# A planned attention and feed-forward kernel: VectorE takes score tiles earlier, half chunks become slices, two weights' homes become buffers, and the plan is made by other rules

## The chip, the cores and the metric

The kernel runs on one core of one Trainium2 chip. A core has TensorE (in profiles PE, its weight loads PEld), ScalarE (ACT), VectorE (DVE), GpSimd (POOL) and SyncE (SP), each with a queue of its own that runs in order. The metric is the device time of one execution in microseconds (us), lower is better.

## The reference

The input is 2048 rows of 640. After a layer norm, an attention with 32 query heads of 20 dimensions that share one key and one value head, and a feed-forward part with silu, 1728 wide, are added to the input.

```python
def reference(A_x, A_wq, A_wk, A_wv, A_wo, B_x, B_w1, B_w2):
    x = A_x                                      # (1, 2048, 640)
    xn = _layernorm(x, axis=-1)
    def _A_ref(x, wq, wk, wv, wo):               # H = 32, Dh = 20
        q = (x @ wq).reshape(B, S, H, Dh).transpose(0, 2, 1, 3)
        k, v = x @ wk, x @ wv                    # one head, Dh wide
        p = _softmax(einsum("bhqd,bkd->bhqk", q, k) * (Dh ** -0.5), axis=-1)
        o = einsum("bhqk,bkd->bhqd", p, v)
        return o.transpose(0, 2, 1, 3).reshape(B, S, H * Dh) @ wo
    def _B_ref(x, w1, w2):                       # w1 640x1728, w2 1728x640
        return _silu(x @ w1) @ w2
    return x + _A_ref(xn, A_wq, A_wk, A_wv, A_wo) + _B_ref(xn, B_w1, B_w2)
```

## The kernel before

**Tiles.** The 2048 queries are four chunks of 512 (QC), the 32 heads eight groups of four (NG, HG), so there are 32 pairs of chunk and group, and each walks over 16 key tiles of 128 (KT). One score tile is 128 keys by 512 queries of one head and fills one PSUM bank; there are 2048. A head's 20 dimensions lie in one of four groups of 32 partitions, so the scores of four different heads can run side by side on TensorE as four matmuls of 32 rows (L1052, function `s_mm`). One to four of them together are called a burst here, and a visit is the time TensorE spends with bursts between other work.

**Two ways to the exponential.** ScalarE takes two or three score tiles from neighbouring banks in one instruction (L1140). VectorE takes one tile at a time (L1336): it adds a bias to the score and writes an int16 whose bits, read as bf16, are a power of two with a straight line between powers. Four such tiles, the four heads of one key tile, are a batch and lie in one buffer of `z_t`. Two shifted copies of the batch are made, by GpSimd (L1375) or VectorE (L1380), and the three are multiplied with three weighted copies of the values, which makes up for the straight lines. So a batch costs three groups of value matmuls (L1175, four matmuls of 32 columns side by side) where ScalarE's tiles cost one. There are five buffers in `z_t`: three of their own and two halves of `zx`.

**Other work on TensorE.** Queries (`q_job`, 20 jobs of 5 groups), hidden layer (`h_job`, `h_pair`), outputs (`out_job`, 24 jobs, and `y_job`, 8 jobs for the last chunk of queries) go through `col_mm` (L434), four matmuls of 32 columns side by side. A hidden job is evicted by ScalarE's tanh (L756) and VectorE (L759), a query job by VectorE (L679), which also sends its rows to their places by DMA (L692), an output job by VectorE (L878 and L893). Of the 14 hidden chunks of 128 the last has 64 live rows; two query chunks share one job for it, so the even one's rows lie in the lower half of the partitions and the odd one's in the upper half, and the other half is zero. An output matmul group can be cut into four slices of 32 rows (`row_slice`, `row_mm`, L441) that run beside a score burst whose heads leave a row group free; slices of one job wait for each other.

**The prologue.** Until `pro` is empty, TensorE takes in order the transposes of the normed rows (L582, copied by L594 or ScalarE L591), the keys (L608, copied by ScalarE L618), the values (L632, L640) and the first two query jobs. In this time ScalarE's banks are fixed: three and two by turns (`ABUFS`), and other jobs have two banks (`XBANKS`); VectorE takes no score tiles.

**The order of the work.** `build` is a planner: it holds a cost for every instruction and a clock for every engine, and always gives the engine that is furthest behind its next instruction. For TensorE, `step_pe` sorts what is ready by kind (s scores for ScalarE, d a score tile for VectorE, r a slice, z a slice left over, p and pd value matmuls, m and l jobs) in an order that depends on the rules: numbers such as `keep`, `hold`, `need`, `stay`. They start from `BASE`, and every 10,000 ns of planned time the next letter of `PLAN` picks an entry of `RULES` that changes some of them. `emit` turns the plan into five queues and semaphore waits, so the chip runs each queue in the planned order. Bank 7 always accumulates the values; the other seven are handed out as they come free.

Of the kernel before, what the change touches and what calls it, by code (L numbers as in the profile page):

```python
# [14 lines left out]
P = 128  # L15
# [21 lines left out]
UB = 7  # L37
XBANKS = (5, 6)
VECTOR_EXP = True
# [41 lines left out]
YC = (0, 0, 3, 3)  # L81
EARLY = 0
WLATE = ("w2a", "wo")
# [12 lines left out]

BASE = dict(hold2=0, bnd=4, pj=6000.0, rows=0, rowmin=3, lagmax=6, lagp=0, lagj=6, openlag=5, late=-0.02, lead=0.01, leadmax=0.02, need=460.0, hold=300.0, dwant=600.0, slack=550.0, dnow=400.0, hungry=0.0, patience=0.0, keep=460.0, open=2, zcap=9, stay=0.0, homes=1, want=1, claim=6)
RULES = dict(a={}, b=dict(keep=0.0), c=dict(lagp=3), d=dict(lagp=5), e=dict(lagp=0), f=dict(patience=200.0), g=dict(dwant=0.0),
             h=dict(zcap=4), i=dict(zcap=3), j=dict(homes=0), k=dict(leadmax=-1.0, lead=-1.0), l=dict(lead=0.08, leadmax=0.1),
             m=dict(need=560.0), n=dict(hold=0.0), o=dict(stay=460.0), p=dict(open=1), q=dict(slack=400.0), r=dict(hungry=1000.0), s=dict(claim=9), t=dict(open=3), u=dict(claim=4), v=dict(want=2), w=dict(slack=700.0), x=dict(hold2=4), y=dict(bnd=0), z=dict(pj=-1e9), A=dict(rows=0), B=dict(rows=2, rowmin=2), C=dict(pj=2000.0), D=dict(openlag=3), E=dict(pj=8000.0), F=dict(hold2=3), G=dict(rows=1))  # L100
PLAN = "aaanGtxBBExhEhmxadrBBzraCBBEGqtrztfFzrqhwnpofocotyxddmGjvmpBaBitntqo"

# [16 lines left out]
class Op:  # L119
    __slots__ = ("eng", "fn", "occ", "lat", "pre", "reads", "writes", "prio", "mode", "slots",  # L120
                 "start", "fin", "done", "deps", "inc", "job", "first", "last", "gate", "on_commit", "seq", "name",
                 "dma_sem", "dma_val", "port", "run", "cut", "ends", "sync")

    def __init__(self, eng, fn, occ, lat=0.0, pre=(), reads=(), writes=(), prio=5.0, mode=None, slots=None,
                 job=None, gate=None, on_commit=None, name=""):
        self.eng = eng
        self.fn = fn
        self.occ = occ
        self.lat = lat
        self.pre = list(pre)  # L130
        self.reads = list(reads)
        self.writes = list(writes)
        self.prio = prio
        self.mode = mode
# [12 lines left out]
        self.port = False  # L147
        self.cut = None
        self.sync = None
        self.ends = (True, True)  # L150

# [167 lines left out]
def build(nc, A_x, A_wq, A_wk, A_wv, A_wo, B_x, B_w1, B_w2, out, stack):  # L319
# [346 lines left out]
    def q_job(qc, k):  # L666
# [5 lines left out]
        for c in range(DC):  # L672
# [4 lines left out]
                     and all(o.done for o in q_piece.get(ql - NQS, ())), dyn=True)  # L677
        xq_read[qc].append(job)
        op = Op("dve", lambda v: v.tensor_scalar_mul(q_st[:, st, :], bk(job.bank), QSCALE), t_dve(512), 140,  # L679
                pre=[job.ready], writes=[res("qst", st)], prio=0.4, job=job)  # L680
# [24 lines left out]
    hc_op = {}  # L705
    xq_read = {k: [] for k in range(QC)}
    t_users = {}
    out_done = {}

    def h_pair(qb):  # L710
# [13 lines left out]
        for q in (qa, qb):  # L724
            xq_read[q].append(job.ops[-1])
        ts = (qb * FC + fk) % 2
        tp = [t_users[ts]] if ts in t_users else []
# [15 lines left out]
    def h_job(qc, fk):  # L743
# [8 lines left out]
        job = pe_job(f"h{qc}_{fk}", mms, 1100, gate=lambda: qc < 2 or all((qc - 2, i) in out_done for i in range(QTP)), dyn=True)  # L752
        xq_read[qc].append(job)
        ts = (qc * FC + fk) % 2
        tp = [t_users[ts]] if ts in t_users else []
# [14 lines left out]
    def load_xres(qc):  # L770
        for i in range(QTP):
# [94 lines left out]
    def out_job(qc, i, hf):  # L866
        e0, e1 = hf * HALF, (hf + 1) * HALF
        mms = ffn_mms(qc, i, e0, e1, True, False) + o_mms(qc, i, e0, e1, False, True)
        job = pe_job(f"out{qc}_{i}_{hf}", mms, 19 * 140, gate=lambda: (qc, NG - 1) in pack_op, dyn=True)
        sl = (QTP * qc + i) % 3  # L870

# [17 lines left out]
    def y_job(qc, i, hf):  # L889
        e0, e1 = hf * HALF, (hf + 1) * HALF  # L890
        mms = ffn_mms(qc, i, e0, e1, True, not YC[i]) + o_mms(qc, i, e0, e1, False, True, range(YC[i]))
        job = pe_job(f"y{qc}_{i}_{hf}", mms, (14 + YC[i]) * 140, dyn=True)
        op = Op("dve", lambda v: v.scalar_tensor_tensor(out=yx[:, i, e0:e1], in0=bk(job.bank, 0, HALF), scalar=0.5,  # L893
                                                        in1=xres[:, i, e0:e1], op0=ALU.mult, op1=ALU.add),
                t_dve(HALF), 140, pre=[job.ready, xres_op[(qc, i)]] + [norm_op[n] for n in range(NT)] + [out_done[(qc - 1, t)] for t in range(QTP)], reads=[res("xres", i)], writes=[res("yx", i, hf)], prio=0.3, job=job)
        y_op[(i, hf)] = op
        job.consumers = [op]
        return job
# [108 lines left out]
    ru = SimpleNamespace(**BASE)  # L1007
    att = {"sgroup": 0, "pgroup": 0, "n": 0, "items": 0, "value": 0.0}
    NGR = QC * NG
# [307 lines left out]
    def yx_users(zi):  # L1317
        return [wqp0] if zi >= NZ0 else []

# [212 lines left out]
    def ready_to_make(m):  # L1532
# [11 lines left out]
        if m[0] == "y":  # L1544
            if (m[1], m[2]) not in xres_op or any((m[1], fk) not in hc_op for fk in range(FC)):
                return False
            return all((m[1] - 1, t) in out_done for t in range(QTP)) and all((m[1], g) in pack_op for g in range((YC[m[2]] * P - 1) // (HG * DH) + 1))
        if m[0] == "h" and m[2] == FC - 1 and m[1] == 3 and not all((0, i) in out_done for i in range(QTP)):
# [104 lines left out]
    def pe_candidates():  # L1653
# [10 lines left out]
        prog = (att["items"] + HG * len(batches)) / total_items  # L1664
        lead = misc_done[0] / misc_total - PACE * prog - ENDLEAD * max(0.0, prog - ENDFROM) / (1.0 - ENDFROM)
        behind = lead < ru.lead or recent() < BUSY
# [28 lines left out]
    def row_slice(piece):  # L1695

        job = piece.job
        if not job.dyn or not ru.rows or sc.pe_mode != "s" or sc.pe_set is None or sc.t["pe"] > sc.pe_set[2] + 1.0 or job.burst == sc.pe_set[0]:
            return None
        busy = sc.pe_set[1]  # L1700
        pick = next(((x, r) for x in job.rest for r in job.rest[x] if r not in busy), None)
        if pick is None and len(job.rest) < ru.rows and len(piece.mms) > ru.rowmin:
            x = next((x for x in list(piece.mms)[-2:0:-1] if x.cut is not None and all(p.done for p in x.pre)), None)
# [53 lines left out]
    def step_pe():  # L1757
# [71 lines left out]
    def commit_pe(e, op, what):  # L1829
# [244 lines left out]
```

## Time and profile before

| | |
|---|---|
| median of 3 runs (693.70 to 693.74) | 693.72 us |
| the profiled execution | 693.9 us |
| its span, first to last instruction | 692.1 us |
| TensorE busy, matmuls | 680.5 us, 98% |
| ScalarE busy | 673.5 us, 97% |
| GpSimd busy | 593.0 us, 86% |
| VectorE busy | 572.0 us, 83% |
| score tiles that VectorE takes (L1336) | 656 of 2048 |
| first and last start of L1336 | 37.1 and 667.2 us |

The page of the profile gives, for each engine, the time in which it had an instruction in flight, the chain of work that ended last, and groups of instructions with their line, engine, operation, shapes, count, busy time, mean duration of one and the idle time before them. A row of the timeline gives start, duration, engine, line and how many instructions are merged in it; square brackets hold the idle time before it and who ended it. A row of a stretch (two times with a colon) gives its length, then busy time and count for each engine asked for, the granted clock, the share of DMA and the GB/s. A wait reads as who waited, for whom, the total in us, the times, the longest. Matmuls are pipelined, so TensorE can be busy without being at its peak.

### The profile page before, as it was taken

The page shows a single profiled execution, that of the slowest core. Times are in us where ns is not written, and L with a number is a line of the kernel's source. Part 1 is how long each engine was busy: PE and PEld are TensorE (multiplying, and loading weights), DVE is VectorE, ACT ScalarE, POOL GpSimd, SP SyncE. Part 2 cuts the span into 40 slices and gives each one's busy share as a digit, 9 for nine tenths or more (in the row PEclk, how much of TensorE's full clock was granted, in tenths as well). Part 3 has the DMA queues.
Part 4 walks back from the last instruction along what each step waited for, and adds up shares of the span by engine and source line. Part 5 has one row for each costly group of instructions (what it writes and reads, how often), then busy time and mean ns, then how long its engine had stood idle before and what let it go on. Part 6 is the DMA issues. An engine that isn't in the chain of part 4 may idle for free.

```text
span 692.1 us, 22655 instructions
## 1 busy us (share of the span) xinstructions
PE 680.5 (98%) x9908; PEld 229.7 (33%) x9911; DVE 572.0 (83%) x977; ACT 673.5 (97%) x727; POOL 593.0 (86%) x355
## 2 busy tenths in 40 slices
PE   8999999999999999999999999999999999999998
PEld 5432222222222333322223333322222333333344
DVE  7788889988988788789989878789898877888843
ACT  6899999999999999999999999999999999999993
POOL 6658999899988789898998879989889999988890
PEclk9999999999999999999999999999999999999999
DMA  8642220222221222233202222122222202232201
GB/s 223 194 158 39 20 22 14 35 33 27 22 19 14 37 39 24 29 74 35 27 9 28 31 29 33 22 63 41 30 20 21 22 19 31 31 68 23 23 7 40
DMA packets 34241, 28.97 MB, mean 42 GB/s; under 512 B 15486, under 2 KB 29662, under 8 KB 34142
## 3 DMA queue, kind: packets, MB, share of 16 engines
q1 hardware_dynamic: 33854, 27.20, 25.5%
q8 instruction: 77, 1.26, 0.7%
q10 hardware_dynamic: 288, 0.33, 0.1%
q14 instruction: 22, 0.18, 0.1%
HBM read 11.09 MB, written 2.62 MB: 20 GB/s over the span
## 4 chain that ended last, share of the span: by engine, by line
ACT 57%; PE 35%; DVE 5%; POOL 3%; issue 1%; DMA 0%
ACT sbt L1140 53%; PE psall L434 11%; PE psall L1175 11%; PE psall L1052 11%; ACT sbt L756 3%; POOL sbt L1375 2%; DVE sbt L1336 1%; DVE sbt L552 1%; DVE sbt L550 1%; DVE sbt L594 1%; POOL sbt L836 0%; DMA sbt<-in_A_x_dram 0%; PE psall L608 0%; PE psall L973 0%; DVE sbt L679 0%
## 5 line engine op out<-in xcount | busy, mean ns | idle before, releaser
L1140 ACT ACTIVATE sbt<-psall 128x1024 bf16<-128x1024 f32 (+1 forms) x655 | 652.5, 1220 | 2.2 <-PE psall L1052 1.7
L1375 POOL TENSOR_SCALAR sbt<-sbt 128x2048 int16<-128x2048 int16 x279 | 530.5, 1901 | 62.7 <-DVE sbt L1380 12.7
L1336 DVE TENSOR_SCALAR sbt<-psall 128x512 int16<-128x512 f32 x656 | 428.8, 684 | 79.6 <-PE psall L1052 72.0
L1052 PE MATMUL psall<-sbt 32*128 32x512 bf16 x2048 | 265.9, 384 | 3.7 <-ACT sbt L1140 1.8
L1175 PE MATMUL psall<-sbt 128*32 128x512 bf16 x3360 | 267.7, 384 | 1.2 <-DVE sbt L1223 0.4
L434 PE MATMUL psall<-sbt 128*32 128x320 bf16 (+2 forms) x3844 | 226.6, 331 | 0.7 <-ACT sbt L1140 0.5
L1052 PEld LDWEIGHTS psall<-sbt 32*128 32x128 bf16 x2048 | 70.0, 91 | 248.8 <-ACT sbt L1140 194.9
L434 PEld LDWEIGHTS psall<-sbt 128*32 128x32 bf16 x3844 | 83.9, 95 | 77.7 <-issue 46.9
L1175 PEld LDWEIGHTS psall<-sbt 128*32 128x32 bf16 x3360 | 66.0, 94 | 115.1 <-issue 82.4
L836 POOL TENSOR_TENSOR sbt<-sbt 128x512 bf16<-128x512 f32 x30 | 38.3, 1276 | 6.8 <-DVE sbt L1380 4.8
L759 DVE SCALAR_TENSOR_TENSOR sbt<-sbt,psall 128x512 bf16<-128x512 bf16 x52 | 35.5, 683 | 5.6 <-ACT sbt L756 4.9
L1380 DVE TENSOR_SCALAR sbt<-sbt 128x2048 int16<-128x2048 int16 x49 | 39.8, 827 | 0.2
L756 ACT ACTIVATE sbt<-psall 128x512 bf16<-128x512 f32 x52 | 39.5, 760 | 0.0
L1223 DVE COPY sbt<-psall 128x512 f32<-128x512 f32 x31 | 21.1, 682 | 2.3 <-PE psall L1175 2.2
L441 PE MATMUL psall<-sbt 32*128 32x320 bf16 (+1 forms) x60 | 20.5, 342 | 0.1
L1648 PE MATMUL psall<-sbt 128*32 128x256 bf16 (+1 forms) x264 | 18.1, 370 | 1.2 <-DVE sbt L474 1.2
L878 DVE SCALAR_TENSOR_TENSOR sbt<-psall,sbt 128x320 bf16<-128x320 f32 x24 | 11.6, 483 | 3.7 <-PE psall L434 2.6
L679 DVE TENSOR_SCALAR sbt<-psall 128x512 bf16<-128x512 f32 x20 | 13.5, 674 | 0.1
L893 DVE SCALAR_TENSOR_TENSOR sbt<-psall,sbt 128x320 f32<-128x320 f32 x8 | 3.9, 485 | 9.8 <-PE psall L434 9.7
L572 POOL TENSOR_SCALAR sbt<-sbt 128x640 bf16<-128x640 bf16 x12 | 10.4, 878 | 1.5 <-DVE sbt L564 1.2
L559 POOL TENSOR_TENSOR sbt<-sbt 128x2 f32<-128x2 f32 x8 | 5.6, 695 | 6.4 <-DVE sbt L557 6.1
L1648 PEld LDWEIGHTS psall<-sbt 128*32 128x32 bf16 x264 | 7.3, 113 | 6.2 <-issue 3.4
(63 smaller groups left out, 111.9 us busy)
## 6 DMA issues: line engine op xcount, KB each, us to landing
sbt<-sbt SPq DMA_DIRECT2D x120, 64.0 KB, 3.8
sbt<-in_A_x_dram SPq DMA_DIRECT2D x28, 160.0 KB, 3.3
sbt<-sbt SPq DMA_DIRECT2D x213, 20.0 KB
out_dram<-sbt SPq DMA_DIRECT2D x14, 160.0 KB, 1.9
sbt<-in_B_w_dram SPq DMA_DIRECT2D x1, 2160.0 KB, 12.7
sbt<-in_B_w_dram SPq DMA_DIRECT2D x1, 2080.0 KB, 8.2
sbt<-sbt SPq DMA_DIRECT2D x75, 8.0 KB
sbt<-in_A_wq_dram SPq DMA_DIRECT2D x1, 800.0 KB, 6.8
```

The costliest lines, as they stand in the source:

```text
L434: ins = pe.matmul(ps[j * SLOT:(j + 1) * SLOT, b * BANK + off:b * BANK + off + n], w[:, j * SLOT:(j + 1) * SLOT], x, start=start, stop=stop ...
L756: t = Op("act", lambda a: a.activation(t_buf[0:rows, ts, :], bk(job.bank, 0, QW, rows=rows), AF.Tanh, scale=0.5), t_act(512), 215, pre=[jo ...
L759: u = Op("dve", lambda v: v.scalar_tensor_tensor(out=hT[par][0:rows, fk, :], in0=t_buf[0:rows, ts, :], scalar=1.0, in1=bk(job.bank, 0, QW, ...
L836: nm = pool(lambda e: e.tensor_tensor(oU[:, us, :], U_sb[:, us, :], Rrep, ALU.mult), 1356.0, pre=[uc] + lc + pack_op.get(divmod(g - 2, NG) ...
L1052: return pe.matmul(bk(b), kT_rep[i * SLOT:(i + 1) * SLOT, kt * P:(kt + 1) * P], qT[i * SLOT:(i + 1) * SLOT, g % NQ, :], start=True, stop=T ...
L1140: return a.activation(Ebuf[:, es * QW:es * QW + w], ps[:, buf[0] * BANK:buf[0] * BANK + w], AF.Exp, scale=ESCALE)
L1175: ins = pe.matmul(ps[i * SLOT:(i + 1) * SLOT, UB * BANK:UB * BANK + QW], lhsT, rhs, start=(first and k < HG), stop=(last and k >= len(lst) ...
L1223: uc = Op("dve", lambda v: v.tensor_copy(U_sb[:, us, :], bk(UB)), t_dve(512), 140, pre=[pv] + up, reads=[sc.banks[UB]], writes=[res("U", u ...
L1336: p1 = Op("dve", lambda v: v.tensor_scalar(z16[:, i * QW:(i + 1) * QW], bk(job.bank), ZBIAS, 0.0, ALU.add, ALU.max), t_dve(QW) + 2.0, 140, ...
L1375: op = pool(lambda v, t=t, j=j, zin=zin: v.tensor_scalar(t.bitcast(I16), zin, float(SHIFT[j]), 1.0, ALU.add, ALU.mult), POOL_SHIFT, 0.0, p ...
L1380: op = dve(lambda v, t=t, j=j, zin=zin: v.tensor_scalar_add(t.bitcast(I16), zin, float(SHIFT[j])), t_dve(N, 4), prio=SPRIO - 0.01 * j, **args)
L1648: ins = pe.matmul(ps[i * SLOT:(i + 1) * SLOT, UB * BANK:UB * BANK + n], zero_t[:, 0:SLOT], zero_t[:, 0:n], start=fresh, stop=fresh, tile_p ...
```

## The change

- `ARUN` gives ScalarE two and two banks in the prologue instead of three and two; `XBANKS` has three banks, 4, 5 and 6.
- `EARLY`, `EARLYN`, `EARLYG`: in the prologue VectorE may take score tiles, once row tile 7 is normed, the queries of group 1 are planned and one of the three banks is free. It takes them from the group after ScalarE's.
- `stay` is 520 in `BASE` (it was 0, and 460 under the letter o): a burst for ScalarE goes to the end of the order while ScalarE has work for more than 230 + 520 ns.
- `half` and `short`: the last hidden chunk of an output job may be cut into slices of its 64 live rows only, two instead of four. `ffn_mms` puts it last but one, so that it isn't the job's last.
- `z_t` gets three more buffers, one in the home of wq and two in that of w1, free once the last matmul that reads the weight is issued (`w_read`, `lent_z`).
- `lagl` and `pace` let the order depend on how far the projections are behind; `y` jobs have another bound on the groups they wait for; new letters H to K; o means `stay` 0.
- The rule string is another, 67 letters instead of 68.

```diff
-XBANKS = (5, 6)
+XBANKS = (4, 5, 6)
+ARUN = ((0, 1), (2, 3))
...
-EARLY = 0
+EARLY = 1
+EARLYN = 7
+EARLYG = 1
...
-BASE = dict(hold2=0, ..., stay=0.0, homes=1, want=1, claim=6)
+BASE = dict(pace=-1.0, lagl=3, half=6, hold2=0, ..., stay=520.0, homes=1, want=1, claim=6)
-             ... o=dict(stay=460.0), ...
+             ... o=dict(stay=0.0), ... H=dict(half=0), I=dict(half=3), J=dict(stay=440.0), K=dict(stay=600.0))
-PLAN = "aaanGtxBBExhEhmxadrBBzraCBBEGqtrztfFzrqhwnpofocotyxddmGjvmpBaBitntqo"
+PLAN = "acJwavcGdxyDytyaxactEnBEaEBhqznBrrxrxnrkyByctaFtrJGmoxwvwawEtyByagz"
...
+    NZ1 = len(z_t)
+    z_t.append(wq_sb[:, :, :].rearrange("p c d -> p (c d)")[:, 0:HG * QW])
+    z_t += [w1f[:, QTP * D + 2 * P + k * HG * QW:QTP * D + 2 * P + (k + 1) * HG * QW] for k in range(2)]
...
+    def short(job, qc):
+        for op in job.ops:
+            if hc_op[(qc, FC - 1)] in op.pre and op.cut is not None:
+                op.rows = tuple(range(HG))[:HG // 2] if qc % 2 == 0 else tuple(range(HG))[HG // 2:]
+        return job
...
-        for fk in range(FC):
+        for fk in [*range(FC - 2), FC - 1, FC - 2]:
...
-            buf = ABUFS[n % 2]
+            buf = ARUN[n % 2]
...
+    lent_z = {}
+    Z_LENT = {NZ1: ("q", QC * DC), NZ1 + 1: ("h", QC * FC), NZ1 + 2: ("h", QC * FC)}
     def z_idle(k):
+        if k in Z_LENT and k not in lent_z:
+            w, n = Z_LENT[k]
+            if len(w_read[w]) < n or not all(o.done for o in w_read[w]):
+                return False
+            lent_z[k] = sc.order["pe"][-1]
...
-        g = att["sgroup"]
+        g = att["sgroup"] + (1 if pro and EARLYG else 0)
...
-        return [wqp0] if zi >= NZ0 else []
+        return [lent_z[zi]] if zi in lent_z else [wqp0] if zi >= NZ0 else []
...
-            return ... all((m[1], g) in pack_op for g in range((YC[m[2]] * P - 1) // (HG * DH) + 1))
+            return ... all((m[1], g) in pack_op for g in range(min((YC[m[2]] * P - 1) // (HG * DH) + 1, NG - 2)))
...
-        if not pro or EARLY and 1 in q_op and all(o.done for o in q_op[1]) and len(xbanks()) >= EARLY:
+        if not pro or EARLY and (EARLYN not in norm_op or norm_op[EARLYN].done) and 1 in q_op and all(o.done for o in q_op[1]) and len(xbanks()) >= EARLY:
...
+        if pick is None and not job.rest and len(piece.mms) > ru.half > 0:
+            x = next((x for x in list(piece.mms)[1:-1] if len(x.rows) < HG and all(p.done for p in x.pre)), None)
+            if x is not None:
+                pick = next(((x, r) for r in x.rows if r not in busy), None)
...
-            order += ["p", "pd", "m", "d", "l"] if lag >= (ru.lagp if cur_job[0] is None else ru.lagj) else ["m", "pd", "p", "d", "l"]
+            order += ["p", "pd", "m", "d", "l"] if lag >= (ru.lagj if cur_job[0] is not None else ru.lagl if att["lead"] < ru.pace else ru.lagp) else ["m", "pd", "p", "d", "l"]
...
-                job.rest[x] = list(range(HG))
+                job.rest[x] = list(x.rows)
```

More of the change, by code (lines that the diff above doesn't have):

```diff
@@ L121 @@
                  "start", "fin", "done", "deps", "inc", "job", "first", "last", "gate", "on_commit", "seq", "name",
-                 "dma_sem", "dma_val", "port", "run", "cut", "ends", "sync")
+                 "dma_sem", "dma_val", "port", "run", "cut", "ends", "sync", "rows")
     def __init__(self, eng, fn, occ, lat=0.0, pre=(), reads=(), writes=(), prio=5.0, mode=None, slots=None,
@@ L149, in __init__ @@
         self.sync = None
+        self.rows = tuple(range(HG))
         self.ends = (True, True)
@@ L869, in out_job @@
         job = pe_job(f"out{qc}_{i}_{hf}", mms, 19 * 140, gate=lambda: (qc, NG - 1) in pack_op, dyn=True)
+        short(job, qc)
         sl = (QTP * qc + i) % 3
@@ L892, in y_job @@
         job = pe_job(f"y{qc}_{i}_{hf}", mms, (14 + YC[i]) * 140, dyn=True)
+        short(job, qc)
         op = Op("dve", lambda v: v.scalar_tensor_tensor(out=yx[:, i, e0:e1], in0=bk(job.bank, 0, HALF), scalar=0.5,
@@ L1546, in ready_to_make @@
                 return False
-            return all((m[1] - 1, t) in out_done for t in range(QTP)) and all((m[1], g) in pack_op for g in range((YC[m[2]] * P - 1) // (HG * DH) + 1))
+            return all((m[1] - 1, t) in out_done for t in range(QTP)) and all((m[1], g) in pack_op for g in range(min((YC[m[2]] * P - 1) // (HG * DH) + 1, NG - 2)))
         if m[0] == "h" and m[2] == FC - 1 and m[1] == 3 and not all((0, i) in out_done for i in range(QTP)):
@@ L1697, in row_slice @@
         job = piece.job
-        if not job.dyn or not ru.rows or sc.pe_mode != "s" or sc.pe_set is None or sc.t["pe"] > sc.pe_set[2] + 1.0 or job.burst == sc.pe_set[0]:
+        if not job.dyn or not (ru.rows or ru.half) or sc.pe_mode != "s" or sc.pe_set is None or sc.t["pe"] > sc.pe_set[2] + 1.0 or job.burst == sc.pe_set[0]:
             return None
@@ L1701, in row_slice @@
         pick = next(((x, r) for x in job.rest for r in job.rest[x] if r not in busy), None)
+        if pick is None and not job.rest and len(piece.mms) > ru.half > 0:
+            x = next((x for x in list(piece.mms)[1:-1] if len(x.rows) < HG and all(p.done for p in x.pre)), None)
+            if x is not None:
+                pick = next(((x, r) for r in x.rows if r not in busy), None)
         if pick is None and len(job.rest) < ru.rows and len(piece.mms) > ru.rowmin:
-            x = next((x for x in list(piece.mms)[-2:0:-1] if x.cut is not None and all(p.done for p in x.pre)), None)
+            x = next((x for x in list(piece.mms)[-2:0:-1] if x.cut is not None and len(x.rows) == HG and all(p.done for p in x.pre)), None)
             r = next((r for r in range(HG) if r not in busy), None)
```

11 lines of the change are left out of this document (8 added, 3 removed).

## The prediction

> **What bounds the kernel now.** I read the page first: busy shares, the slices, the chain that ended last.
>
> ```profile
> span 692.1 us, 22655 instructions
> PE 680.5 (98%) x9908; PEld 229.7 (33%) x9911; DVE 572.0 (83%) x977; ACT 673.5 (97%) x727; POOL 593.0 (86%) x355
> ACT 57%; PE 35%; DVE 5%; POOL 3%; issue 1%; DMA 0%
> ```
>
> The reader is to see two engines without room and two with some: ScalarE (ACT) and TensorE (PE) share the chain, VectorE (DVE) is idle for 120 us. The profiled execution took 693.9 us, its span 692.1 us; the median of the three runs is 693.72 us, 0.2 us below it. I make the sum against the span and put 1.6 us on top.
>
> Next the groups, shapes kept apart, then the waits.
>
> ```profile
> L1140 ACT ACTIVATE sbt<-psall 128x1024 bf16<-128x1024 f32 x573 | 555.0, 1172 | 0.3
> L1336 DVE TENSOR_SCALAR sbt<-psall 128x512 int16<-128x512 f32 x656 | 428.8, 684 | 79.6 <-PE psall L1052 72.0 <-PE psall L441 3.0
> L1175 PE MATMUL psall<-sbt 128*32 128x512 bf16 x3360 | 267.7, 384 | 1.2 <-DVE sbt L1223 0.4 <-DVE sbt L1380 0.4
> L1052 PE MATMUL psall<-sbt 32*128 32x512 bf16 x2048 | 265.9, 384 | 3.7 <-ACT sbt L1140 1.8 <-ACT sbt L618 0.2 <-DVE sbt L616 0.2
> L1140 ACT ACTIVATE sbt<-psall 128x1536 bf16<-128x1536 f32 x82 | 124.6, 1555 | 1.9 <-PE psall L1052 1.7
> L434 PE MATMUL psall<-sbt 128*32 128x512 bf16 x1440 | 113.5, 383 | 0.6 <-ACT sbt L1140 0.3
> L434 PE MATMUL psall<-sbt 128*32 128x320 bf16 x2288 | 109.8, 301 | 0.2 <-ACT sbt L1140 0.2
> ...
> L441 PE MATMUL psall<-sbt 32*128 32x320 bf16 x32 | 9.7, 304 | 0.0
> PEld psall L1052 <- ACT sbt L1140: 194.9, 503, 0.8
> ```
>
> All work comes down to 2048 score tiles (L1052). ScalarE exponentiates 573x2 + 82x3 = 1392 of them in 655 instructions, VectorE the other 656 (L1336), and it waits for scores 72 us in all. How PE spends its time is in the timeline.
>
> ```profile
> 299.46 7.03 ACT L1140 ACTIVATE sbt<-psall 128x1024 bf16<-128x1024 f32 x7
> 299.81 0.39 PE L1052 MATMUL psall<-sbt 32*128 32x512 bf16 x3
> 300.13 0.61 PE L1175 MATMUL psall<-sbt 128*32 128x512 bf16 x8
> 300.68 0.46 PE L1052 MATMUL psall<-sbt 32*128 32x512 bf16 x4
> 666.18 0.62 PE L1175 MATMUL psall<-sbt 128*32 128x512 bf16 x8
> 667.05 1.05 PE L1175 MATMUL psall<-sbt 128*32 128x512 bf16 x16
> 673.59 1.13 PE L434 MATMUL psall<-sbt 128*32 128x320 bf16 x28
> 676.23 0.73 PE L434 MATMUL psall<-sbt 128*32 128x320 bf16 x16
> ```
>
> Four matmuls are one group side by side. Two more groups of 512 columns take 1.05 - 0.62 = 0.43 us, so 0.215 us each; three more of 320 columns 1.13 - 0.73 = 0.40 us, so 0.133 us each. A score burst is also one pass of 512 columns, but from its start to the next group go 0.32 us, and from the start of two groups to the next burst 300.68 - 300.13 = 0.55 us instead of 0.43. So each visit to the scores costs 0.105 us going in and 0.12 us coming out beyond its pass. With 655 visits (one per ScalarE instruction) PE needs 655 x 0.44 = 288 us for scores, 3360/4 x 0.215 = 181 us for L1175, 1440/4 x 0.215 = 77 us and 2288/4 x 0.133 = 76 us for L434: 622 us, and some 40 us for everything that isn't in these rows (estimate: the smaller groups, fillers and prologue matmuls among them). That is 662 us of 692: at most 30 us are to be had from PE by better order alone, some of them in the first and last 10 us.
>
> **The exchange rate.** Tiles per stretch, by the windows view of L1052:
>
> ```profile
> 100.00:200.00 100.00, 40.07 (x306) 10.77 (x306) 1.00 0.22 26
> 200.00:300.00 100.00, 41.03 (x324) 10.67 (x324) 1.00 0.26 36
> 300.00:400.00 100.00, 41.66 (x313) 11.24 (x310) 1.00 0.23 27
> 400.00:500.00 100.00, 39.64 (x314) 10.29 (x314) 1.00 0.27 37
> 500.00:600.00 100.00, 40.10 (x313) 10.67 (x313) 1.00 0.22 24
> ```
>
> 1570 tiles in 500 us, 3.14 per us: a tile finished outside this stretch is worth 0.32 us of the end.
>
> **The change, part by part.**
>
> *Head tiles in the prologue (EARLY, EARLYN, EARLYG, XBANKS, ARUN).*
>
> ```profile
> 30.73 0.39 SPq L1438 DMA_DIRECT2D sbt<-in_B_w_dram  x1
> 30.65 0.89 DVE L594 COPY sbt<-psall 128x640 bf16<-128x640 bf16 x2 [0.71 <-PE psall L582]
> 32.22 0.89 DVE L594 COPY sbt<-psall 128x640 bf16<-128x640 bf16 x2 [0.68 <-PE psall L582]
> 35.99 0.54 DVE L640 TENSOR_SCALAR sbt<-psall 128x80 bf16<-128x80 f32 x3 [2.88 <-PE psall L632]
> 37.14 2.05 DVE L1336 TENSOR_SCALAR sbt<-psall 128x512 int16<-128x512 f32 x3 [0.61 <-PE psall L1052]
> 22.08 6.89 ACT L1140 ACTIVATE sbt<-psall 128x1536 bf16<-128x1536 f32 x6 [0.49 <-PE psall L1052]
> 35.88 0.64 ACT L618 ACTIVATE sbt<-psall 128x512 bf16<-128x512 f32 x1
> 41.07 3.88 POOL L1375 TENSOR_SCALAR sbt<-sbt 128x2048 int16<-128x2048 int16 x2 [8.02 <-DVE sbt L1336]
> L1140 ACT ACTIVATE sbt<-psall 128x1536 bf16<-128x1536 f32 x9 | 13.1, 1460 | 1.5 <-PE psall L1052 1.5
> L1140 ACT ACTIVATE sbt<-psall 128x1024 bf16<-128x1024 f32 x9 | 9.3, 1039 | 0.0
> ```
>
> The early tiles need the queries of group 1. The DMA of L1438 waits for the same queries and leaves at 30.73 us, so VectorE can begin there instead of at 37.14. In between it stands 0.71 + 0.68 + 2.88 + 0.61 = 4.88 us; at 2.05/3 = 0.68 us per tile that is 7 tiles, x 0.32 = -2.2 us. They join bursts that are there, so PE's scores cost nothing; their shifts fall into POOL's 8.02 us of standing before 41 us, and no DMA comes with them. Their later groups of L1175, two more per four tiles, replace ScalarE visits (below). Against it: with two banks per ScalarE instruction instead of three and two by turns, an instruction covers less PE work. The last two rows are ScalarE's instructions of the first 37 us: nine three-wide and nine two-wide, 45 tiles. A two-wide one passes in 1.0 us (7.03/7), the mix in 6.89/6 = 1.15; each wait for scores may grow by that 0.15, at five places: +0.7 us. Sum -1.5 us. Ends: -2.2, and +4.4 if the first rival's price comes.
>
> *The half chunk as slices (half, short, rows).* The last hidden chunk has 64 live rows of 128. Each of 24 output and 8 y jobs gives up one group of 320 columns, 32 x 0.133 = 4.3 us, and gets two slices of 32 rows that run beside a burst. Before, 32 such slices ran already (L441, 320 columns; four for one group), 1.1 us. So 3.2 us of PE are left to free. Both slices of a chunk write one bank and wait for each other, so a job of 19 groups (2.6 us, about three visits) must find two bursts that leave the right row group free; a burst uses two to four of the four. I take three quarters: -2.5 us. Ends: -3.2, and +2 (a slice left over gets a visit of its own: 0.44 - 0.133 = 0.3 us, seven times).
>
> The Trainium skill, "TensorEngine Tiling (Array Packing)", section Restrictions and Gotchas, says that different row tiles can't write the same PSUM bank at the same time. The code keeps to it, and no run here shows what happens otherwise: were the rule not there, both slices could ride in one burst and the term would be the whole -3.2 us; with it, -2.5.
>
> *Late bursts (stay 520).* A burst is put off while ScalarE has more than 230 + 520 = 750 ns ahead; the old rule hold = 300 with need = 460 already puts off two-wide bursts over 760 ns ahead. And 503 of 655 bursts wait for the bank that ScalarE gives back (194.9 us above): they are late already. 0 us; ends -2 (fuller bursts) and +2 (ScalarE's 2.2 us of waiting for scores doubled).
>
> *Lent homes (wq, w1).*
>
> ```profile
> L756 ACT ACTIVATE sbt<-psall x52: 591/757/917, 49.3 to 530.1; 128x512 bf16<-128x512 f32 x52
> L679 DVE TENSOR_SCALAR sbt<-psall x20: 627/681/693, 15.9 to 483.2; 128x512 bf16<-128x512 f32 x20
> 500.00:600.00 100.00, 67.75 (x104) 1.00 0.22 24
> ```
>
> The last query job is evicted at 483 us and the last hidden job at 530 us; only then are the buffers free. VectorE's tiles run at 104 in these 100 us (last row, L1336), and 656 in some 630 us is 104 too: no sign that five buffers hold it back. -0.5 us; ends 0 and -2 (six tiles more).
>
> *No effect.* lead falls below pace = -1 only with no projection done at the very end, so lagl never acts. The y gate's min(5, NG - 2 = 6) is the old 5. Two matmuls of a chunk change places: 0.
>
> *The rule string.* It orders everything from 0 to 680 us anew, and no row prices its letters. Bounds from the stretches: all at the best one's 324 tiles, 3.2% of the 630 us between 40 and 670, -20 us; all at the worst one's 306, +16 us. PE's 30 us of slack and VectorE's 72 us of waiting leave room to go up; nothing shows where. I take a third of the way from the mean to the best, 1% or -6.3 us: the likelier sign, since the slices and late buffers give the order more to choose from, and near the mean, which the five rows crowd.
>
> *Sum:* -1.5 - 2.5 + 0 - 0.5 - 6.3 = -10.8 us: span 681.3 us, time 682.9 us. It should come with 25 to 35 more tiles on VectorE: 10.8 us of ScalarE at 0.5 us a tile is 22, and the slack eaten on PE the rest.
>
> **The rivals.**
>
> *The prologue pays more than it gains (slower, chance 0.17).* ScalarE's 45 tiles of the first 37 us are 23 visits in twos instead of 18, 5 x 0.225 = 1.1 us of PE in a stretch where every PE job is on the way to the last keys. VectorE's early tiles (7 x 0.68 = 4.8 us) can go ahead of the copies of L594, which the keys wait for; if all of it lands there the prologue ends 4.8 us later. With ScalarE's 0.7 us more that is 6.6 us against 2.2 gained and the string at 0: +4.4 - 2.5 = +1.9, 695.6 us. It decides as soon as the prologue loses over 4.7 us and the string gives nothing; against a string that gives 6.3 us it would have to lose 11. For it: VectorE (third pair) is 87% busy between 20 and 30 us. Against it: the 4.88 us above.
>
> ```profile
> 20.00:30.00 10.00, 9.59 (x128) 4.56 (x128) 8.72 (x33) 8.26 (x9) 7.27 (x10) 1.00 0.63 226
> ```
>
> *The named parts only (faster, chance 0.20).* The string gives 0: -4.5 us, 689 us. For it: ACT 97% and PE 98% leave an order little to find.
>
> *All of PE's slack is found (faster, chance 0.10).* The best stretch's rate everywhere, -20 us, in place of 6.3: 669; with half of it 676. I set 673 us. Against it: POOL, busy 593 us, must take two shifts of 1.9 us per four tiles more, and the end's 12 us hold no tile.
>
> *PE's freed time is worth nothing (faster, chance 0.08).* If the 30 us of slack lie all along the kernel, PE is no bound and ScalarE alone sets the end: the slices' 2.5 us drop out, -8.3 us, 685.4 us. For it: 194.9 us in which weights wait for ScalarE. Against it: 662 of 692 us are passes and switches. The Trainium skill, "Trainium Kernel Development and Optimization", section Performance Expectations, says matmul busy time is a bad measure of the distance to the limit, because matmuls are pipelined. The trace agrees as far as that 30 us of slack hide in the 98%.
>
> *It does nothing (within 0.2%, chance 0.05).* The gains and the prologue's loss cancel: 693 us. A change of 0.2%, 1.4 us, is about what this kernel's runs can tell.
>
> **How the numbers follow.** The forecast, 682.9 us, has 0.40 with its own range 677 to 688. Faster: 0.40 + 0.20 + 0.10 + 0.08 = 0.78; same 0.05; slower 0.17. For 8 in 10 the range goes from 674 (most of the rival in which all slack is found lies below it) to 695 (above it lies over half of the first): 0.08 and 0.10 left out.
>
> **What will show it.** L1336 starts near 31 us and has 4 to 8 tiles before 37; ScalarE's instructions before 36 us are all two-wide; its last key copy (L618) ends no later than 36.5 + 0.7 us. The 320-column L441 goes from 32 to about 64 with 320-column L434 down by some 100. L1336 count 680 to 690, L1140 tiles down as many. Tiles per 100 us near 317. If instead L1336 counts 656 and the stretches still hold 314, the string term fails; if L618 ends after 41 us, the prologue rival has come. Long waits of L1175 for a POOL shift would be a cause that I haven't counted.

## The result

The changed kernel takes 705.5 us (median of four runs, 704.9 to 706.4), the kernel before 693.71 us on the same chip: 1.67% slower, ratio 1.0167 with an interval of 1.0154 to 1.018. Forecast was 682.9 us, faster. The profiled execution took 705.94 us, its span 704.1 us, 12.0 us more than before.

First the page's busy shares and chain of the changed kernel, in the order in which the prediction shows them.

```profile
span 704.1 us, 22566 instructions
...
PE 681.5 (97%) x9886; PEld 230.6 (33%) x9889; DVE 556.5 (79%) x945; ACT 683.5 (97%) x725; POOL 595.9 (85%) x357
...
ACT 71%; PE 21%; POOL 3%; DVE 2%; DMA 2%; SPq 1%; issue 0%; DVEq 0%; POOLq 0%
```

TensorE is busy for as long as before (681.5 against 680.5 us) and stands 11 us more. ScalarE is busy 10.0 us longer, and the rest of its span grows from 18.6 to 20.6 us: together the 12 us. VectorE works 15.5 us less. The groups and waits say what ScalarE has more of (lines of the changed file: L1160 is the exponential, L1364 VectorE's tile, L1072 the scores, L441 and L448 the column matmuls and the slices, L1676 fillers).

```profile
L1160 ACT ACTIVATE sbt<-psall 128x1024 bf16<-128x1024 f32 x547 | 531.8, 1169 | 5.1 <-PE psall L1072 4.6
L1364 DVE TENSOR_SCALAR sbt<-psall 128x512 int16<-128x512 f32 x636 | 422.6, 687 | 104.2 <-PE psall L1072 98.0 <-PE psall L448 1.6
L1160 ACT ACTIVATE sbt<-psall 128x1536 bf16<-128x1536 f32 x106 | 158.6, 1602 | 0.5 <-PE psall L1072 0.5
L441 PE MATMUL psall<-sbt 128*32 128x320 bf16 x2212 | 109.6, 301 | 1.2 <-DMA sbt<-sbt 0.9 <-ACT sbt L1160 0.3
L448 PE MATMUL psall<-sbt 32*128 32x320 bf16 x62 | 18.9, 305 | 0.0
...
L1676 PE MATMUL psall<-sbt 128*32 128x512 bf16 x156 | 14.2, 386 | 0.0
L1676 PE MATMUL psall<-sbt 128*32 128x256 bf16 x172 | 8.9, 330 | 1.2 <-DVE sbt L481 1.2
```

ScalarE takes 547x2 + 106x3 = 1412 tiles, 20 more than before, and VectorE 636, 20 fewer than before. With all its work counted ScalarE is busy 0.484 us per tile in both kernels (673.5 us by 1392 and 683.5 by 1412), so the 20 tiles are its 10 us, and the tiles themselves didn't get slower; VectorE's takes 687 ns against 684. VectorE gets its scores later: it waits 98.0 us for them instead of 72.0. Fillers, matmuls on zeros that the plan gives TensorE where it has nothing ready for a while, went from 264 (116 and 148 of L1648 before) to 328.

Where along the kernel? Score tiles by stretch, first the changed kernel, then the first two rows of the kernel before (its rows from 100 to 600 us are in the prediction).

```profile
0.00:50.00 50.00, 13.40 (x93) 3.60 (x93) 1.00 0.67 197
50.00:100.00 50.00, 18.63 (x147) 4.97 (x144) 1.00 0.26 29
100.00:200.00 100.00, 37.96 (x298) 10.05 (x298) 1.00 0.20 24
200.00:300.00 100.00, 38.82 (x309) 10.22 (x309) 1.00 0.27 36
300.00:400.00 100.00, 42.18 (x310) 11.38 (x310) 1.00 0.23 26
400.00:500.00 100.00, 39.01 (x313) 10.31 (x313) 1.00 0.26 36
500.00:600.00 100.00, 39.00 (x306) 10.19 (x306) 1.00 0.20 24
```

```profile
0.00:50.00 50.00, 13.03 (x88) 3.28 (x88) 1.00 0.67 198
50.00:100.00 50.00, 19.82 (x151) 5.21 (x151) 1.00 0.23 25
```

The first 50 us are better, 93 tiles against 88, but by 100 us the lead is gone: the next 50 us have 4 fewer, and a single window from 0 to 100 us holds 237 against 239. From 100 to 600 us the rows add up to 1536 against 1570, fewer in each stretch. A tile that crosses the edge of a stretch counts in both; in one window from 100 to 600 us there are 1536 against 1567, 31 fewer, x 0.32 = 9.9 us. The loss is in every stretch, but not evenly: 8 and 15 of the rows' 34 tiles are lost between 100 and 300 us, then 3, 1 and 7.

### The profile page after: what moved, and what is told of

The parts are those of the page before. It is cut to its first block, busy times and chain, and to the rows that moved or that the text cites. A ratio compares the mean times of both kernels' runs of the same rounds, so it can differ in the third digit from the quotient of the medians.

```text
span 704.1 us, 22566 instructions
## 1 busy us (share of the span) xinstructions
PE 681.5 (97%) x9886; PEld 230.6 (33%) x9889; DVE 556.5 (79%) x945; ACT 683.5 (97%) x725; POOL 595.9 (85%) x357
## 4 chain that ended last, share of the span: by engine, by line
ACT 71%; PE 21%; POOL 3%; DVE 2%; DMA 2%; SPq 1%; issue 0%; DVEq 0%; POOLq 0%
ACT sbt L1160 68%; PE psall L1072 7%; PE psall L1195 6%; PE psall L441 6%; ACT sbt L767 3%; POOL sbt L1403 1%; DMA sbt<-sbt 1%; DMA sbt<-in_A_wk_dram 0%; DVE sbt L1364 0%; PE psall L589 0%; POOL sbt L854 0%; DVE sbt L961 0%; PE psall L615 0%; SPq L867 0%; POOL sbt L566 0%
## 5 line engine op out<-in xcount | busy, mean ns | idle before, releaser
L1160 ACT ACTIVATE sbt<-psall 128x1024 bf16<-128x1024 f32 (+1 forms) x653 | 660.4, 1239 | 5.7 <-PE psall L1072 5.1
L1364 DVE TENSOR_SCALAR sbt<-psall 128x512 int16<-128x512 f32 x636 | 422.6, 687 | 104.2 <-PE psall L1072 98.0
L1072 PE MATMUL psall<-sbt 32*128 32x512 bf16 x2048 | 264.6, 385 | 9.0 <-ACT sbt L1160 5.4
L1195 PE MATMUL psall<-sbt 128*32 128x512 bf16 x3320 | 262.7, 384 | 2.8 <-DVE sbt L1243 0.9
L441 PE MATMUL psall<-sbt 128*32 128x320 bf16 (+3 forms) x3784 | 230.1, 332 | 2.4 <-ACT sbt L1160 0.9
L1072 PEld LDWEIGHTS psall<-sbt 32*128 32x128 bf16 x2048 | 69.9, 91 | 245.6 <-ACT sbt L1160 168.5
L441 PEld LDWEIGHTS psall<-sbt 128*32 128x32 bf16 x3784 | 82.6, 95 | 83.1 <-issue 49.4
L1195 PEld LDWEIGHTS psall<-sbt 128*32 128x32 bf16 x3320 | 68.7, 94 | 118.3 <-issue 75.5
L767 ACT ACTIVATE sbt<-psall 128x512 bf16<-128x512 f32 x52 | 37.5, 722 | 0.3 <-PE psall L441 0.3
L1408 DVE TENSOR_SCALAR sbt<-sbt 128x2048 int16<-128x2048 int16 x37 | 28.8, 788 | 1.0 <-PE psall L1195 0.8
L1676 PE MATMUL psall<-sbt 128*32 128x256 bf16 (+1 forms) x328 | 22.6, 356 | 1.2 <-DVE sbt L481 1.2
L448 PE MATMUL psall<-sbt 32*128 32x320 bf16 (+1 forms) x74 | 23.5, 318 | 0.1
L1676 PEld LDWEIGHTS psall<-sbt 128*32 128x32 bf16 x328 | 8.9, 106 | 8.9 <-issue 5.7
```

Source lines behind the costliest of these rows:

```text
L441: ins = pe.matmul(ps[j * SLOT:(j + 1) * SLOT, b * BANK + off:b * BANK + off + n], w[:, j * SLOT:(j + 1) * SLOT], x, start=start, stop=stop ...
L448: return pe.matmul(ps[0:w.shape[-1], b * BANK:b * BANK + n], w[k], x[k], start=start, stop=stop, tile_position=(r * SLOT, 0))
L767: t = Op("act", lambda a: a.activation(t_buf[0:rows, ts, :], bk(job.bank, 0, QW, rows=rows), AF.Tanh, scale=0.5), t_act(512), 215, pre=[jo ...
L1072: return pe.matmul(bk(b), kT_rep[i * SLOT:(i + 1) * SLOT, kt * P:(kt + 1) * P], qT[i * SLOT:(i + 1) * SLOT, g % NQ, :], start=True, stop=T ...
L1160: return a.activation(Ebuf[:, es * QW:es * QW + w], ps[:, buf[0] * BANK:buf[0] * BANK + w], AF.Exp, scale=ESCALE)
L1195: ins = pe.matmul(ps[i * SLOT:(i + 1) * SLOT, UB * BANK:UB * BANK + QW], lhsT, rhs, start=(first and k < HG), stop=(last and k >= len(lst) ...
```

## The experiments

Two theories. **String:** the kernel before owed its time to a rule string that fits its planner, letter after letter, and the new string isn't such a fit for the new planner; the features themselves cost little or gain. **Feature:** one of the new features (late bursts, slices, the prologue, lent buffers) costs the 12 us. All times are medians; the kernel before stood at 693.7 to 694.6 us beside them.

**The string away, or exchanged.** e1 and e2 are the two kernels with

```diff
-PLAN = "..."
+PLAN = ""
```

> The kernel before with an empty rule string: every piece runs under BASE. String theory (the old kernel owed its time to a string that fits its own plan, piece by piece, and the new string doesn't fit the new plan as well): the fit is lost, 702 to 712 us, with more standing of PE and fewer tiles on VectorE. Feature theory (one of the new features costs the 12 us, the string is worth little): 692 to 698 us.

> The changed kernel with an empty rule string, to be read against the kernel before with an empty string. String theory: without a string the features cost nothing, within 6 us of the kernel before with an empty string. Feature theory: 10 us or more above it.

e1 took 709.9 us, e2 709.7 us. Without a string the kernel before loses 16 us, and the features make no difference that the runs can tell. Then each kernel gets the other's string; the kernel before needs one more rule for it, and the letter o means in each kernel what it meant there (460 before, 0 in the changed one).

```diff
-..., G=dict(rows=1))
-PLAN = "aaanGtxBBExhEhmxadrBBzraCBBEGqtrztfFzrqhwnpofocotyxddmGjvmpBaBitntqo"
+..., G=dict(rows=1), J=dict(stay=440.0))
+PLAN = "acJwavcGdxyDytyaxactEnBEaEBhqznBrrxrxnrkyByctaFtrJGmoxwvwawEtyByagz"
```

> The kernel before with the new rule string (letter J, stay 440, added to its rules; o keeps its old meaning). String theory: 703 us or more, since a string fits one planner only. Feature theory: 692 to 698 us, the features being out.

> The changed kernel with the old rule string (o now means stay 0). String theory: 702 us or more, the old string doesn't fit the new plan either. If the old string were good in itself, whatever the planner: 685 to 692 us. Feature theory: 704 to 707 us as now.

e3 took 725.7 us, e4 711.8 us. So neither string is good in itself: the old one that gives 693.7 us on its planner gives 711.8 on the new one, and the new one, 705.5 us on its planner, gives 725.7 on the old. The busy shares of e1 and e3 show that TensorE's share doesn't tell a bad plan from a good one:

```profile
span 708.6 us, 22638 instructions
...
PE 686.5 (97%) x9936; PEld 230.5 (33%) x9939; DVE 532.7 (75%) x907; ACT 690.7 (97%) x732; POOL 610.6 (86%) x365
```

```profile
span 724.3 us, 23146 instructions
...
PE 699.4 (97%) x10204; PEld 238.3 (33%) x10207; DVE 528.2 (73%) x898; ACT 696.5 (96%) x731; POOL 594.6 (82%) x356
```

Both have TensorE at 97%, while the kernel before, 32 us faster than the second, has 98%. VectorE is the engine that tells them apart, 83% in the kernel before against 75% and 73%.

**One feature undone at a time, with the new string.**

```diff
# e5: late bursts off
-..., stay=520.0, ... o=dict(stay=0.0)
+..., stay=0.0, ... o=dict(stay=460.0)
# e6: the old prologue
-XBANKS = (4, 5, 6); ARUN = ((0, 1), (2, 3)); EARLY = 1
+XBANKS = (5, 6); ARUN = ((0, 1, 2), (3, 4)); EARLY = 0
# e7: no half slices of their own
-..., half=6, ...
+..., half=0, ...
# e8: no lent buffers, in z_idle
+        if k in Z_LENT:
+            return False
```

> The changed kernel and its string, late bursts taken out (stay 0 in BASE, 460 under o). Late-burst theory (put-off bursts let VectorE and PE stand): back towards 694 us, VectorE's waiting for scores from 98 towards 72 us. String theory: another arbitrary plan, 698 to 712 us, no return to 694.

> The changed kernel and its string with the old prologue (EARLY 0, banks three and two, two banks for other jobs). Prologue theory: back by what the prologue lost, 694 to 700 us. String theory, and what the trace of the change shows (93 score tiles in the first 50 us against 88): no gain, 703 to 712 us, and 5 tiles fewer in the first 50 us.

> The changed kernel and its string with half 0, so half chunks are cut only where a letter asks for rows. Slice theory (slices crowd VectorE's tiles out of the bursts): back towards 694 us, and more VectorE tiles than 636. String theory: 2 to 3 us more PE work in 320-column groups and another arbitrary plan, 702 to 714 us.

> The changed kernel and its string without the three lent buffers. They come free after the last query and hidden jobs, so nothing before some 490 us can differ from the changed kernel. Lent theory (later buffers upset the end): 694 to 700 us. String theory: 702 to 708 us, the first 480 us as in the changed kernel.

They took 706.0, 707.0, 713.4 and 707.1 us. In e5 two letters J and one o of the new string still set `stay` to 440 and 460 for 10 us each; elsewhere it is 0. None goes back towards 694; undone, each feature leaves the time where it was or makes it worse, so no single one of them carries the loss. The feature theory falls, in its form with one culprit. The sizes aren't the features' worth, since each run is also another plan. What can be read from them is what happens before the plans part: e6 has 88 tiles in its first 50 us, as the kernel before, against 93. e8, which can't differ before the lent buffers come free, has VectorE's tiles as the changed kernel until 480 us, 242 each from 50 to 300 us and 185 against 184 from there, and the time differs by 1.6 us in the end, 0.1% when each is set against the kernel before in its own session (ratios 1.0178 and 1.0167).

**One letter.** If a string is a fit, changing one letter can spoil all that follows.

```diff
# e9: the kernel before, letter for 340 to 350 us
-PLAN = "...GqtrztfFzrq..."
+PLAN = "...GqtrzttFzrq..."
# e10: the changed kernel, letter for 400 to 410 us
-PLAN = "...xnrkyByctaF..."
+PLAN = "...xnrkgByctaF..."
```

> The kernel before with one letter of its string changed, the one for 340 to 350 us (f to t). String theory: the first 340 us as before (tiles, VectorE's share), and from there every later letter meets another state, so that the fit is lost for the rest: 6 to 16 us slower, 700 to 710 us. If a letter only matters in its own 10 us: within 2 us of 693.7.

> The changed kernel with one letter of the new string changed, the one for 400 to 410 us (y to g). If the new string fits its planner as the old one fits the old: slower by 6 to 16 us, 711 to 721 us. If it is an ordinary string there: as likely faster as slower, 697 to 712 us.

e9 took 711.5 us, 17.6 us more for a letter that rules 10 us; 16 was the most that was expected. VectorE's tiles in three stretches, the kernel before and e9:

```profile
40.00:340.00 300.00, 206.36 (x317) 1.00 0.24 31
340.00:500.00 160.00, 107.16 (x166) 1.00 0.25 32
500.00:650.00 150.00, 101.58 (x155) 1.00 0.22 28
```

```profile
40.00:340.00 300.00, 206.41 (x317) 1.00 0.24 31
340.00:500.00 160.00, 98.03 (x149) 1.00 0.24 31
500.00:650.00 150.00, 84.72 (x128) 1.00 0.21 27
```

The same 317 tiles until 340 us, then 17 and 27 fewer in these stretches; in the end 636 against 656. ScalarE is busy 9.1 us longer for it (682.6 us) and stands 8.7 us longer. The loss doesn't stay in the letter's own 10 us: the letters behind, unchanged, met another state. That is the prediction's error in one pair. e10 took 702.7 us, 2.8 us *faster*. Both letters were picked with the planner's own count, e10's as one that it counts as a gain, so the two aren't a fair sample of letters, and what an average letter is worth no run shows; but a string in which one other letter gains 2.8 us isn't fitted to the end.

**Are the features worth something with equal strings?** Two strings drawn at random from the letters that both kernels know (e11 and e12, e13 and e14), and one pair of strings put together anew for each planner with equal effort (e15, e16).

```diff
-PLAN = "..."
+PLAN = "wjBmDzEBxtaEqCgxaFdamrGgnuavgaBfpjdGCndCDacwwqccaGafCfdGdklfuFyxfdzfFn"    # e11, e12
+PLAN = "kampdcjalkEwvawyzlakmEkrzldrrzdajaBmGnauDpmnvEaqazdwfaCgEqmtmFtjCqavBC"    # e13, e14
+PLAN = "aaanxpFxaxBGlxlaFmvmrmGcpdDvzxoxxrzrqzqfoqaqfxxojxpxrprryvpvvvamzavBCaa"    # e15, before
+PLAN = "aaavGdxdxxtxvFzwwzzHzwczKggonGaBxlJznzpBaBgootxoxzxJhBzpoGBtcomarEEvza"    # e16, changed
```

> The kernel before with a string drawn at random from the letters that both kernels know, to be read against the changed kernel with the same string. Both theories of the string: far above 693.7, 705 to 725 us.

> The changed kernel with the same drawn string. If the features are worth what the prediction gave the named parts, 4.5 us less than the kernel before with that string, with a spread of 5 us either way from the order; if they cost the 12 us, 12 us more.

> The kernel before with a second drawn string, to be read against the changed kernel with the same one. Far above 693.7: 705 to 720 us.

> The changed kernel with the second drawn string. If the features are worth some 5 us with any ordinary string: 0 to 10 us less than its partner; if they cost the 12 us: 12 us more.

> The kernel before with a string put together anew for its planner, letter after letter, the twenty best beginnings kept at each step. It tells how much of 693.7 is the string's: between an ordinary 710 and 694, so 695 to 708 us.

> The changed kernel with a string put together for its planner in the same way and with the same effort. String theory: the fit is what was missing, faster than 705.5, 693 to 703 us, and if the features are worth some 5 us with equal strings, that much under its partner. Feature theory: no string brings it near, 705 us or more.

| string | before | changed | difference |
|---|---|---|---|
| empty (e1, e2) | 709.9 | 709.7 | -0.2 |
| drawn (e11, e12) | 719.4 | 713.6 | -5.8 |
| drawn (e13, e14) | 710.4 | 710.5 | +0.2 |
| fitted with equal effort (e15, e16) | 707.3 | 700.9 | -6.4 |
| the old one (before, e4) | 693.7 | 711.8 | +18.1 |
| the new one (e3, changed) | 725.7 | 705.5 | -20.2 |

In the four pairs whose strings favour neither side the features gain 3.0 us on average, from +0.2 to -6.4; the second drawn pair misses its expectation, 0 to 10 us less, by that 0.2. Under such strings they don't cost 12 us. That they gain is not shown, with four pairs that spread over 6.6 us. The last two pairs show the size of what a string that suits one planner does: 18 and 20 us.

Two things stay open. The effort behind e15 gets back only 2.6 of the 16 us that the old string is worth, and no run shows how that string was found. And no run has a string for the changed planner that is as good as the old one is for its own (e16, 700.9 us, is the best): that the features cost nothing under ordinary strings doesn't prove that the new planner has one at 694 us.

e16's row for VectorE, beside the changed kernel's above, has the same 636 tiles and nearly the same waiting; its span is 4.9 us shorter because ScalarE is busy 1.9 us less and stands 3.0 us less (681.6 of 699.2 us).

```profile
span 699.2 us, 22769 instructions
...
PE 683.9 (98%) x9993; PEld 228.0 (33%) x9993; DVE 556.8 (80%) x947; ACT 681.6 (97%) x732; POOL 591.9 (85%) x355
...
L1364 DVE TENSOR_SCALAR sbt<-psall 128x512 int16<-128x512 f32 x636 | 423.8, 686 | 104.0 <-PE psall L1072 97.0 <-PE psall L448 2.8
```

**Beside the old string.** e17 keeps the kernel before and its first 60 letters and has others behind them. e18 has the lent buffers as its only feature, the old string's first 48 letters, in which the buffers can't be used yet, and letters picked anew behind; the half chunk keeps its new place and the `y` jobs their new bound, but no half chunk is cut in two slices (24 slices, for 6 groups of columns).

```diff
# e17
-PLAN = "...otyxddmGjvmpBaBitntqo"
+PLAN = "...otyxddmGjvmpBiljhwttggiEtj"
# e18: EARLY 0, the old banks, half 0, stay 0 and o 460 as before, lent buffers in
-PLAN = "...qhwnpofocotyxddmGjvmpBaBitntqo"
+PLAN = "...qhwnpofocoCycdEqGavmpzaopantqctzaia"
```

> The kernel before with its string kept for the first 600 us and other letters for the last 90, picked out of many for its planner. String theory: the old string is already close to the best that can be found at its end, so 691.5 to 694 us; that it beats 693.7 by more than 0.2% is not expected, by 0.1% is.

> The kernel before with the three lent buffers alone (other features off), the old string for the first 480 us, in which the buffers can't be used, and letters picked anew for its planner behind that. So the fit of the first 480 us is kept and only this feature is new. If more buffers late are worth 0.5 us as predicted or up to 2: 691.5 to 694 us; if they are worth nothing and the picked end is a little worse than the old one: 694 to 696 us.

e17 took 693.47 us beside 694.07 of the kernel before: ratio 0.999, interval 0.9982 to 0.9999. It is 0.1% faster than the kernel before, barely clear of the noise. e18 took 695.32 us, ratio 1.0019 (1.001 to 1.0028). VectorE's tiles in e18, with the kernel before's behind:

```profile
40.00:480.00 440.00, 300.00 (x461) 1.00 0.24 31
480.00:600.00 120.00, 75.95 (x115) 1.00 0.23 26
600.00:690.00 90.00, 49.53 (x74) 1.00 0.18 25
```

```profile
40.00:480.00 440.00, 300.07 (x461) 1.00 0.24 31
480.00:600.00 120.00, 81.20 (x125) 1.00 0.23 26
600.00:690.00 90.00, 45.25 (x69) 1.00 0.18 27
```

Equal until 480 us, and then 10 tiles fewer and 5 more: with a fit kept up to the point where they come free, three more buffers bring no more tiles, 652 in all against 656. Whether a better end exists for them is open.

**The plan's own length.** One rival is left: that the new plan is the shorter one on paper, and the chip departs from it. `build` can be run without a chip, and the latest end of an instruction in its plan is 689.9 us for the kernel before and 701.3 us for the changed one: 11.4 us apart, where the measured spans are 12.0 us apart. In all twenty kernels here the span of the profiled execution is 0.2 to 4.3 us longer than the plan. So the chip follows the plan, the new plan is the longer one, and a sign of this size stood in the kernels' own source before any run. Differences of under some 4 us can't be read from it: by the plan e2 is 2.1 us longer than e1, by the span it is 0.5 us shorter.

## Why the prediction was wrong

*The rule string, the step that failed.* The prediction put it at -6.3 us, "a third of the way from the mean to the best" of five stretches, with "the likelier sign" upward. The runs lead from the one kernel to the other in three steps: the old string taken away, +16.2 us (e1); the features put in, -0.2 us (e2); the new string put in, -4.2 us, to 705.5 us. On this path the string's term is +12.0 us and the named parts' -0.2 us, where the prediction had -6.3 and -4.5. By the other equal-string pairs the features are worth +0.2 to -6.4 us, so that of the 11.8 us lost in all the string's term would be +12 to +18 us.

The error lies in what the stretches are samples of. All five come from a kernel whose string fitted, and they don't show what another order gives: the changed kernel's own five have a mean of 307, near the worst of the five before (306), and e1's and e3's have means of 304 and 299, beyond it. The kernel before with other strings or one letter changed took 707 to 726 us (e1, e3, e9, e11, e13, e15), never less than 13 us above 693.7, but for e17, which keeps 60 letters; the changed kernel with other strings took 701 to 714 us (e2, e4, e10, e12, e14, e16). The term should have been "the old fit is lost, unless the new string is as good": +16 us by e1, less what the new string recovers, 4.2 us by e2. The prediction looked for a price in the rows, where "no row prices its letters"; the two plans' own lengths, 11.4 us apart, price them together with the features.

The slow bound that the prediction worked out for it, all at the worst stretch's 306 tiles, +16 us, was close, but it got no rival and no chance of its own. That this bound and the named parts' -4.5 us add up to nearly 705.5 us is luck: the -4.5 us is not seen in the end.

The prediction's own signs said so too. It expected 680 to 690 tiles on VectorE and near 317 per 100 us, and named 656 and 314 as the sign that the string gives nothing; 636 and 307 came, the other side of that.

*Head tiles in the prologue, -1.5 us.* Right for the first 50 us, and not kept. First tile at 33.2 us, not 31; four by 37 us, where the sum had seven; 93 tiles against 88 at 50 us, 5 x 0.32 = -1.6 us. At 100 us it is 237 against 239, and e6, with the old prologue and the new string, has 237 too: nothing of the term is left where the next stretch begins. ScalarE's first 22 instructions are two-wide and it waits 2.1 us before them instead of 1.5, +0.6 where 0.7 was set. In the timeline of the changed kernel stand the last key copy (L625) and the early tiles, in the groups of its first 37 us ScalarE's instructions:

```profile
35.89 0.65 ACT L625 ACTIVATE sbt<-psall 128x512 bf16<-128x512 f32 x1
33.17 1.29 DVE L1364 TENSOR_SCALAR sbt<-psall 128x512 int16<-128x512 f32 x2
34.74 1.29 DVE L1364 TENSOR_SCALAR sbt<-psall 128x512 int16<-128x512 f32 x2 [0.28 <-PE psall L1072]
```

```profile
L1160 ACT ACTIVATE sbt<-psall 128x1024 bf16<-128x1024 f32 x22 | 20.8, 1038 | 2.1 <-PE psall L1072 2.0
```

The last key copy starts at 35.89 us, 35.88 before. So the rival that ended on the right side, slower, was wrong in its mechanism: the last key copy isn't later, and the prologue itself cost nothing. (Its 695.6 us leaves out the lent homes' -0.5 us; with it the sum is 695.1.)

*Half chunks as slices, -2.5 us.* Right as work taken off TensorE: 62 slices (64 set), and 2288 - 2212 = 76 column matmuls fewer ("some 100" set), 19 groups x 0.133 = 2.5 us: by these counts 23 half chunks in two slices each and 4 other groups in four, where 8 groups were cut in four before. Against that, 4 groups of 512 columns that ran as slices before run whole now (1456 - 1440 matmuls), 0.9 us. Whether that reaches the end no run shows by itself; e7, with 2292 of them again, is 7.9 us slower, more than the work, by its other plan.

*Late bursts, 0.* Nothing speaks against it: 706.0 us without them, VectorE's waiting for scores 95.8 us against 98.0, within what another plan does.

*Lent homes, -0.5 us.* Not shown either way: e18, with the fit kept until 480 us and other letters behind, is 0.2% slower; e8, which takes the buffers away, has 4 VectorE tiles fewer and is 0.1% slower. Both are the size of what another plan does. The prediction's own reading, that nothing in the rows shows five buffers to be short, leads to 0 rather than -0.5.

*What bounds the kernel.* That TensorE and ScalarE are the engines without room agrees with every run: they are busy 95 to 98% of the span in all twenty profiles. The price of a visit holds as well: in the timelines from 40 to 660 us the median way from a burst of three to the next group is 0.32 us in both kernels. By the prediction's prices the changed kernel has less for TensorE to do (653 x 0.44, 3320/4 and 1456/4 x 0.215, 2212/4 x 0.133: 618 us against 622), yet it ends 12 us later, so what was lost is order and not work. That 30 us were to be had on TensorE is not shown, since no span here is under 691.5 us; and slack doesn't say in which direction an order will move. The rival in which TensorE's freed time is worth nothing isn't settled.

## What to carry to other kernels

A plan made by a list scheduler with rules per stretch of time is a chain in which every decision rests on the state that the ones before left: one letter for 10 us of 690, picked with the planner's count, cost 17.6 us. Where a change alters anything the planner sees, run the planner and compare the lengths of the two plans first. Where that can't be done, price the change against plans with ordinary rules, not against the tuned plan's own stretches, and count the loss of the old fit as a term with its full size. To judge features, compare them under several strings that favour neither side, or search both with equal effort.

## What the runs showed that was not expected

TensorE's busy share hardly moves with the time: 98% at 693.7 us, 97% at 725.7 us, with 680.5 us busy in the kernel before and 681.5 us in the one that is 12 us slower. The engine with room, VectorE, carries the information: 82 and 83% busy in the two fastest kernels (e17 and the kernel before), 73% in the two slowest (e3 and e11). Its share alone doesn't give the time either: e12 with 648 VectorE tiles took 713.6 us, e16 with 636 took 700.9, since the loss also shows as ScalarE standing (span 711.8 us, busy 679.7, in e12).
